# The opening of a Linformer attention and maxout FFN kernel: another form of one projection, other places for two sums, and loads cut in halves

## The chip, the cores and the metric

The kernel runs on one core of a Trainium2 chip. A core has five engines that work beside each other, each through its own instructions in order: TensorE (PE; loading its weights has a row of its own, PEld), VectorE (DVE), ScalarE (ACT), GpSimd (POOL) and SyncE (SP). The last two issue most of the DMAs here. TensorE writes into PSUM, which this kernel treats as eight banks of 128 x 512 f32. The metric is device time in microseconds, the median over runs.

## The reference, cut to what matters

```python
k_proj = np.einsum('ks,bhsd->bhkd', E, k)
v_proj = np.einsum('ks,bhsd->bhkd', F, v)
scores = scale * np.matmul(q, k_proj.transpose(0, 1, 3, 2))
attn = softmax(scores)            # over the 64 projected places
x = (attn @ v_proj)               # heads side by side: 8192 x 512
h = np.maximum(np.maximum(x @ w1, x @ w2), x @ w3)
out = h @ w_out
```

There are 8 batches, 8 heads, a sequence of 1024 and a head dimension of 64. E and F project the sequence onto 64 places. The FFN goes from 512 to 768 and back to 512. Inputs and outputs are f32.

## The kernel before, in words

**Tiling.** The sequence is split as 128 partitions by 8 places (`SI`), the heads into four pairs (`g` = 0 to 3), the 512 columns of x into the same four pieces (`ct`, one for each pair of heads), and the 768 of the FFN into six (`jt`). A batch has two chunks of 512 rows (four of the eight places each). For a chunk, x transposed (`xT`) times a weight gives a product of 128 x 512: 3 weights x 6 `jt` x 4 `ct` = 72 products (`up_mm`, L668), followed by 24 products with `w_out` (L776).

**Order.** The order on every engine is the order of the Python calls; nothing is rescheduled (`manual_schedule`, L60). A planner's clock (`clock`, `pe`, `runs`, `at`) does no more than choose PSUM banks: `bank` and `two` take those that by its count come free first. What it gets wrong turns into a wait of TensorE for the engine that still reads the bank.

**The opening, batch 0** (L631 to L661, then `up_first`, L681). The inputs come in pieces, through GpSimd's DMA queue, in the order of use: q and k by halves of the heads, v by pairs, then the weights by pieces of `ct`. Idle products (`idle`) keep TensorE busy meanwhile. `k_duo(u)` projects k for two pairs of heads: eight matmuls of 64 rows out and 256 columns (L575), copied by VectorE, and `kt_duo(u)` turns the result with two transposes (L588) and copies it into `kpT`. `v_pair(g)` projects v for one pair (L601). `exps` of `scores` (L221, L232) gives the unnormalized weights `pT`; `z(g)` adds them up (`sums`, L241) and inverts the sums on ScalarE as exp(-ln) (L301, L307); `x(g)` multiplies `pT` with v (L241 again) and scales by the inverse on VectorE into `xT` (L318). The first half of the sequence (`C0`) goes this way, pair by pair; the second half goes through `Duo` later, inside the FFN's products.

`up_first` runs the products of the first weight with `ct` outermost, so that pieces of x can be used as they come: (0, ct, jt) for ct 0 and 1 with jt 0 to 3, then both with jt 4 and 5, then ct 2 and 3. The dictionary handed to it says which attention step follows which product, for instance (before):

```python
(0, 0, 1): [lambda: x(1)],
(0, 0, 3): [lambda: z(2), lambda: z(3)],
(0, 1, 1): [lambda: v_pair(2)],
(0, 1, 3): [lambda: x(2)],
(0, 1, 5): [lambda: v_pair(3), ld(1)],
```

**Loads of the later batches.** `load(b, which)` (L198) issues one DMA for each of q, k and v of a batch, 1 MB each as landed in bf16, on GpSimd's queue. `q_t` has two buffers, `k_t` and `v_t` one, so k of batch 1 waits until batch 0's projections have read theirs. `qd(b)` packs q (copies on VectorE or ScalarE) and has SyncE issue DMAs that transpose it into `qT` (L424). For batch 1 `qd` is called twice, by two pairs each. `kproj(1)` and `vproj(1)` (through `proj`, L355, two column tiles of 64) and the scores of batch 1 stand in chunk 1 of batch 0, as `plan(0)` has them.

Of the kernel before, what the change touches and what calls it, by code (L numbers as in the profile page):

```python
# [9 lines left out]
BF16 = mybir.dt.bfloat16  # L10
# [5 lines left out]
def kernel(  # L16
# [13 lines left out]
    nc = tc.nc  # L30

    B, H, S, D = q.shape
# [5 lines left out]
    P = 128  # L38
    HALF = 64
    SI = 8  # L40
# [5 lines left out]
    SPC = SI // NCHUNK  # L46
# [5 lines left out]
    att = ctx.enter_context(tc.tile_pool(name="att", bufs=2))  # L52
# [18 lines left out]
    def deal(ns):  # L71
        clock["pe"] = max(clock["pe"], *(free[n] for n in ns))
        for n in ns:
            assert free[n] < OPEN
            free[n] = OPEN

    def two():
        n = min(range(0, 8, 2), key=lambda n: max(free[n:n + 2]))
        deal((n, n + 1))
        return psum_t[:, n:n + 2, :], (n, n + 1)  # L80

    def bank():
        n = min(range(8), key=lambda n: free[n])
        deal((n,))
        return psum_t[:, n, :], (n,)

    def pe(dt, wait=0.0):
        clock["pe"] = max(clock["pe"], wait) + dt
        return clock["pe"]

    def runs(eng, ready, dt, ns=()):
        if eng in clock:
            clock[eng] = max(clock[eng], ready + 0.06) + dt
            for n in ns:
                free[n] = clock[eng]
            return clock[eng]
        return ready + dt
# [3 lines left out]
    def copy(eng, o, i, ns=(), dt=0.65):  # L101
        done = {  # L102
            "v": nc.vector.tensor_copy, "s": nc.scalar.copy, "g": nc.gpsimd.tensor_copy
        }[eng](out=o, in_=i)
        runs(eng, clock["pe"] if ns else 0.0, dt, ns)
        return done

    def after(dma, earlier):
        tc.add_manual_dep(
            dma.ins, earlier.ins.name,  # L110
            mybir.DependencyInfo(
                mybir.DependencyClass.Sync, mybir.DependencyReason.DATA
            ),
        )


    def view(src, b):
        return src[b].rearrange("h (p si) d -> p h si d", si=SI)


    ident = const.tile([P, P], BF16, name="ident")
# [9 lines left out]
    qkv, qTs, kpTs, vps, pTs, zis, xTs = {}, {}, {}, {}, {}, {}, {}  # L131
# [5 lines left out]
    def load_tiles(b):  # L137
        qkv[b] = tuple(
            loads.tile([P, H, SI, D], BF16, name=nm, bufs=n)
            for nm, n in (("q_t", 2), ("k_t", 1), ("v_t", 1))  # L140
        )
        return qkv[b]
# [37 lines left out]
    for hp in range(2):  # L180
        for c in range(2):
            at = hp * 16 + c * 8
# [12 lines left out]
    load_w(2, slice(2, 4))  # L195
    nc.gpsimd.dma_start(out=wout_sb, in_=moe_w_out.rearrange("(jt p) m -> p jt m", p=P))

    def load(b, which):  # L198
        tiles = qkv[b] if b in qkv else load_tiles(b)
        for i in which:  # L200
            dma = nc.gpsimd.dma_start(out=tiles[i], in_=view((q, k, v)[i], b))  # L201
            if i == 0 and b - 1 in last_T:
                after(dma, last_T[b - 1])
            if i == 0 and b - 1 in turned:
                after(dma, turned[b - 1])

    def k_pair(b, g):
        if b in turned:
            return kpTs[b][:, g % 2, (g // 2) * KP:(g // 2 + 1) * KP]
        return kpTs[b][:, g, :]  # L210
# [3 lines left out]
    def scores(b, g, lo, nsi):  # L214
        t, ns = two()
        n = nsi // 2
        for c in range(2):
            for hp in range(2):
                rows = slice(hp * HALF, (hp + 1) * HALF)
                at = g * SI + lo + c * n  # L220
                nc.tensor.matmul(  # L221
                    out=t[c * HALF:(c + 1) * HALF, hp, 0:n * P],
                    lhsT=k_pair(b, g)[rows],
                    rhs=qTs[b][rows, at:at + n, :],
                    start=True, stop=True,
                )
        return t[:, :, 0:n * P], ns, pe(n * MM / 4 + 0.1)

    def exps(b, g, lo, nsi, sc):
        t, ns, ready = sc  # L230
        pTs[b, g, lo] = att.tile([P, 2, CHUNK], BF16, name="pT", bufs=6)[:, :, 0:nsi * HALF]
        nc.scalar.activation(out=pTs[b, g, lo], in_=t, func=AF.Exp, scale=scale)  # L232
        runs("s", ready, 0.17 + nsi * 0.107, ns)
# [117 lines left out]
    def proj(b, kv, t, heads, width):  # L351

        for si in range(SI):
            for hh in range(2):
                nc.tensor.matmul(  # L355
                    out=t[hh * HALF:(hh + 1) * HALF, 0:width],
                    lhsT=efT[:, si, (kv - 1) * KP:kv * KP],
                    rhs=qkv[b][kv][:, heads[hh], si, :],
                    start=(si == 0), stop=(si == SI - 1),
                )  # L360
        pe(8 * (width * 0.00042 + 0.01))
# [180 lines left out]
    def idle(n, w=warm):  # L542

        t, ns = bank()
        for _ in range(n):
            nc.tensor.matmul(out=t, lhsT=w[:, 0:P], rhs=w, start=True, stop=True)  # L546
        free[ns[0]] = pe(n * MM * (4 if w is warm_f else 1))
# [19 lines left out]
    def at(us):  # L567
        clock["pe"] = max(clock["pe"], us)

    kp0 = {}  # L570

    def k_duo(u):
        t, ns = bank()
        for si in range(SI):
            nc.tensor.matmul(  # L575
                out=t[0:KP, 0:4 * D], lhsT=efT[:, si, 0:KP],
                rhs=k_t[:, 4 * u:4 * u + 4, si, :],
                start=(si == 0), stop=(si == SI - 1),
            )
        pe(0.9)  # L580
        kp0[u] = att.tile([KP, 4 * D], BF16, name="kp0")
        copy("v", kp0[u], t[0:KP, 0:4 * D], ns, 0.45)

    def kt_duo(u):
        t, ns = bank()
        t = t.bitcast(BF16)
        for gg in range(2):
            nc.tensor.transpose(  # L588
                out=t[:, gg * KP:(gg + 1) * KP],
                in_=kp0[u][:, gg * P:(gg + 1) * P], identity=ident[0:KP, 0:KP],  # L590
            )
        pe(0.15)
        copy(
            "v", kpTs[0][:, 2 * u:2 * u + 2, :].rearrange("a g k -> a (g k)"),
            t[:, 0:2 * KP], ns, 0.25,
        )

    def v_pair(g):
        t, ns = bank()
        for si in range(SI):  # L600
            nc.tensor.matmul(  # L601
                out=t[:, 0:2 * D], lhsT=efT[:, si, KP:3 * KP],
                rhs=v_t[:, 2 * g:2 * g + 2, si, :],
                start=(si == 0), stop=(si == SI - 1),
            )
        pe(0.5)
        copy(
            "v", vps[0][:, 2 * g:2 * g + 2].rearrange("a h d -> a (h d)"),
            t[:, 0:2 * D], ns, 0.3,
        )  # L610
# [14 lines left out]
    def z(g):  # L625
        invert(0, g, *C0, sums(0, g, *C0))

    def x(g):
        scale_x(0, g, *C0, values(0, g, *C0))
# [18 lines left out]
    z(1)  # L648
    idle(1)
    at(12.8)  # L650
    k_duo(1)
    idle(1)
    at(14.8)
    v_pair(0)
    kt_duo(1)
    x(0)
    for g in (2, 3):
        exps(0, g, *C0, scores(0, g, *C0))
    at(16.1)
    v_pair(1)  # L660
    at(17.4)  # L661

    ffn_sb = ctx.enter_context(tc.tile_pool(name="ffn_sb", bufs=2))
    hTs = {}
# [138 lines left out]
    def store_now():  # L803
        stores.pop()()

    def ld(b, which=(0, 1, 2)):
        return lambda: load(b, which)

    def plan(b):
        n = b + 1  # L810
# [59 lines left out]
    for b in range(B):  # L870
        p = plan(b)

        def behind(ch, step):
            for f in p.get((ch, step), []):
                f()

        for ch in range(NCHUNK):
            if (b, ch) == (0, 0):
                c1 = (SPC, SPC)
                up_first({  # L880
                    (0, 0, 1): [lambda: x(1)],
                    (0, 0, 3): [lambda: z(2), lambda: z(3)],
                    (0, 1, 1): [lambda: v_pair(2)],
                    (0, 1, 3): [lambda: x(2)],
                    (0, 1, 5): [lambda: v_pair(3), ld(1)],
                    (0, 2, 1): [lambda: x(3)],
                    (2, "a", 0): [pack_q(0, (0, 1), *c1)],
                    (2, "a", 1): [pack_q(0, (2, 3), *c1)],
                    (2, "a", 3): [qp(0, (0, 1), *c1)],
                    (2, "a", 5): [qp(0, (2, 3), *c1)],  # L890
                    (2, 1): [duo[0].scores],
                    (2, 4): [
                        duo[0].sums, duo[0].values, duo[1].scores, duo[0].invert,
                    ],
                })
                run_later()
                behind(0, NJT - 1)
            else:
                for step in range(NJT):
                    up(b, ch, step, lambda: behind(ch, (step, "mid")))  # L900
                    behind(ch, step)
            for tt in range(SPC):
                down(b, ch, tt, "v" if b == 0 else "s")
                behind(ch, NJT + tt)
# [30 lines left out]
```

## Time and profile before

| | |
|---|---|
| median of 4 runs | 399.07 us (398.81 to 400.12) |
| the profiled execution, by the same clock | 400.12 us |
| its span in the profile | 398.3 us |
| granted TensorE clock | 1.0 |
| first projection of k (L575) | 10.47 us |
| first FFN product (L668) | 18.15 us |
| `kproj(1)`, `vproj(1)` | 50.36 and 57.30 us |
| scores of batch 1 | 56.75 us |

Issue and landing of the loads that the text uses, from the list of DMA issues by time:

| load | issued | us to landing |
|---|---|---|
| first quarter of the first weight | 6.32 | 11.7 |
| the rest of batch 0's q | 19.05 | 12.6 |
| q of batch 1 | 22.67 | 20.2 |
| k of batch 1 | 23.87 | 23.7 |
| v of batch 1 | 25.75 | 28.9 |

In the profile's rows a matmul has a start and a duration that includes the way through the array; products that follow each other start about 0.22 us apart while each is shown with 0.38. A bracket names the idle time of the engine ahead of an instruction and what ended it. "128*64" is the part of the array that an instruction uses.

### The profile page before, as it was taken

What the parts mean: (1) busy time and instruction counts of PE and PEld (TensorE: products, weight loads), DVE (VectorE), ACT (ScalarE), POOL (GpSimd) and SP (SyncE); (2) the same over time, 40 slices, a digit from 0 to 9 for tenths busy, and PEclk for the clock granted to TensorE, in tenths of its full rate; (3) what the DMA queues carried; (4) which work ended last, traced back from release to release, by engine and by line L of the source; (5) the groups of instructions that cost most, each with busy time, mean ns of one, the idle gap of its engine ahead of it and who ended that gap; (6) DMA issues with size and microseconds to landing.
All of it is one profiled execution on the core that took longest, in us unless ns stands there. A gap on an engine that the chain in (4) does not pass through costs nothing.

```text
span 398.3 us, 5745 instructions
## 1 busy us (share of the span) xinstructions
PE 390.7 (98%) x2286; PEld 176.3 (44%) x2286; DVE 202.0 (51%) x312; ACT 152.3 (38%) x239; POOL 34.2 (9%) x49
## 2 busy tenths in 40 slices
PE   7899999999999999999999999999999999999996
PEld 3444443453445445344454445444454444444443
DVE  2348756751864535645273544745266442745251
ACT  2434638527222552253323532245323533132322
POOL 7440011000400200200002000200000000000000
PEclk9999999999999999999999999999999999999999
DMA  8999999977999999999979979696980129020203
GB/s 140 205 206 207 205 253 149 249 139 168 224 181 265 153 221 203 223 179 196 221 207 144 253 166 274 93 229 125 214 215 30 77 76 246 0 105 2 105 0 107
DMA packets 67339, 66.31 MB, mean 166 GB/s; under 512 B 31504, under 2 KB 59792, under 8 KB 67312
## 3 DMA queue, kind: packets, MB, share of 16 engines
q0 software_dynamic: 29104, 30.41, 47.7%
q1 hardware_dynamic: 38064, 35.46, 34.8%
q8 instruction: 18, 0.29, 0.3%
q10 hardware_dynamic: 144, 0.07, 0.1%
q14 instruction: 9, 0.07, 0.0%
HBM read 69.73 MB, written 16.97 MB: 218 GB/s over the span
## 4 chain that ended last, share of the span: by engine, by line
PE 90%; DMA 6%; DVE 1%; ACT 1%; issue 0%; POOL 0%; DVEq 0%; ACTq 0%; POOLq 0%
PE banks L668 60%; PE banks L776 19%; DMA qT<-q_p 4%; PE banks L355 3%; PE banks L241 2%; DMA k_t<-in_k_dram 2%; PE banks L221 2%; PE banks L266 1%; DVE xT L318 1%; ACT zi_all L307 1%; ACT zl L301 1%; PE banks L575 1%; PE banks L546 0%; PE banks L601 0%; PE banks L756 0%
## 5 line engine op out<-in xcount | busy, mean ns | idle before, releaser
L668 PE MATMUL banks<-xT,w_sb 128*128 128x512 bf16 x1152 | 257.1, 379 | 0.3 <-DVE xT L318 0.3
L668 PEld LDWEIGHTS <-w_sb 128*128 128x128 bf16 x1152 | 110.2, 98 | 136.6 <-issue 8.5
L737 DVE TENSOR_TENSOR m<-banks,h1s 128x512 f32<-128x512 f32 x90 | 62.1, 690 | 134.5 <-ACT h1s L733 90.7
L733 ACT COPY h1s<-banks 128x512 f32<-128x512 f32 x90 | 52.6, 585 | 122.2 <-PE banks L668 120.7
L776 PE MATMUL banks<-wout_sb,hT 128*128 128x512 bf16 x378 | 86.9, 380 | 0.1
L678 DVE TENSOR_TENSOR hT<-banks,m 128x512 bf16<-128x512 f32 x90 | 62.3, 692 | 9.4
L776 PEld LDWEIGHTS <-hT 128*128 128x128 bf16 x378 | 35.3, 98 | 48.2 <-issue 5.9
L102 ACT COPY o_sb<-banks 128x512 f32<-128x512 f32 (+2 forms) x57 | 32.9, 577 | 58.6 <-PE banks L776 58.1
L318 DVE TENSOR_TENSOR xT<-banks,zi_all 128x1024 bf16<-128x1024 f32 x28 | 33.2, 1220 | 11.5 <-PE banks L241 6.9
L232 ACT ACTIVATE pT<-banks 128x1024 bf16<-128x1024 f32 (+1 forms) x32 | 30.2, 975 | 15.5 <-PE banks L221 15.5
L201 POOL DMA_DIRECT2D q_t<-in_q_dram x7 | 6.1, 878 | 197.8 <-DVE xT L318 76.7
L355 PEld LDWEIGHTS <-efT 128*64 128x64 bf16 x224 | 11.6, 110 | 3.4 <-issue 3.4
L102 DVE CAST vp<-banks 64x256 bf16<-64x256 f32 (+1 forms) x18 | 7.1, 397 | 11.5 <-ACT vp L102 9.0
L102 ACT CAST vp<-banks 64x256 bf16<-64x256 f32 x14 | 5.1, 364 | 18.4 <-PE banks L355 18.3
L241 PE MATMUL banks<-pT,vp 64*64 64x512 bf16 (+1 forms) x128 | 10.3, 375 | 0.2 <-DVE vp L102 0.2
L221 PE MATMUL banks<-qT,kpT 64*64 64x512 bf16 (+1 forms) x128 | 9.7, 372 | 0.7 <-DMA qT<-q_p 0.7
L102 DVE COPY q_p<-q_t 128x1024 bf16<-128x1024 bf16 x26 | 9.8, 438 | 0.6 <-DMA q_t<-in_q_dram 0.6
L102 DVE COPY o_sb<-banks 128x512 f32<-128x512 f32 (+1 forms) x9 | 5.6, 640 | 5.4 <-PE banks L756 4.5
L546 PE MATMUL banks<-warm_f 128*128 128x512 f32 x8 | 6.6, 977 | 1.5 <-DVE warm_f L175 1.5
L301 ACT ACTIVATE zl<-banks 128x512 f32<-128x512 f32 (+1 forms) x8 | 6.5, 810 | 2.9 <-PE banks L241 2.7
L355 PE MATMUL banks<-k_t,efT 128*64 128x256 bf16 x112 | 7.5, 276 | 0.0
L355 PE MATMUL banks<-v_t,efT 128*64 128x256 bf16 x112 | 7.3, 273 | 0.0
(73 smaller groups left out, 124.3 us busy)
## 6 DMA issues: line engine op xcount, KB each, us to landing
out_dram<-o_sb SPq DMA_DIRECT2D x30, 512.0 KB, 4.5
zi_all<-zd SPq DMA_DIRECT2D x20, 512.0 KB, 7.8
q_t<-in_q_dram POOLq DMA_DIRECT2D x7, 1024.0 KB, 10.2
k_t<-in_k_dram POOLq DMA_DIRECT2D x7, 1024.0 KB, 16.6
v_t<-in_v_dram POOLq DMA_DIRECT2D x7, 1024.0 KB, 21.8
zi_all<-zd POOLq DMA_DIRECT2D x4, 512.0 KB, 7.9
w_sb<-in_moe_w_dram POOLq DMA_DIRECT2D x4, 384.0 KB, 10.4
k_t<-in_k_dram POOLq DMA_DIRECT2D x2, 512.0 KB, 9.5
```

What stands on the lines that cost most here:

```text
L102: done = {"v": nc.vector.tensor_copy, "s": nc.scalar.copy, "g": nc.gpsimd.tensor_copy}[eng](out=o, in_=i)
L221: nc.tensor.matmul(out=t[c * HALF:(c + 1) * HALF, hp, 0:n * P], lhsT=k_pair(b, g)[rows], rhs=qTs[b][rows, at:at + n, :], start=True, stop= ...
L232: nc.scalar.activation(out=pTs[b, g, lo], in_=t, func=AF.Exp, scale=scale)
L241: nc.tensor.matmul(out=t[hp * HALF:(hp + 1) * HALF, c, 0:nsi * HALF], lhsT=w(rows, hp), rhs=p[rows, hp, :], start=True, stop=True,)
L301: nc.scalar.activation(out=zl, in_=t, func=AF.Ln)
L318: nc.vector.tensor_tensor(out=xTs[b][:, g, lo:lo + nsi, :].rearrange("a (c s) p -> a c (s p)", c=2), in0=t, in1=zi, op=ALU.mult,)
L355: nc.tensor.matmul(out=t[hh * HALF:(hh + 1) * HALF, 0:width], lhsT=efT[:, si, (kv - 1) * KP:kv * KP], rhs=qkv[b][kv][:, heads[hh], si, :], ...
L668: nc.tensor.matmul(out=h, lhsT=w_sb[i][:, ct, jt * P:(jt + 1) * P], rhs=xTs[b][:, ct, ch * SPC:(ch + 1) * SPC, :], start=(ct == first), st ...
L678: nc.vector.tensor_tensor(out=o, in0=h, in1=other, op=ALU.max)
L733: nc.scalar.copy(out=h1s, in_=h[0][0])
L737: nc.vector.tensor_tensor(out=m12, in0=h[1][0], in1=h1s, op=ALU.max)
L776: nc.tensor.matmul(out=o_ps, lhsT=hTs[b, ch][:, jt, tt * P:(tt + 1) * P], rhs=wout_sb[:, jt, :], start=(jt == 0), stop=(jt == NJT - 1),)
```

## The change

Three edits. First, `k_quad` and `kt_quad` take the place of `k_duo(1)` and `kt_duo(1)` for pairs 2 and 3 of batch 0. The projection writes two pairs of heads as two column tiles of 64, the lower pair onto partitions 0 to 63, the upper onto 64 to 127, through the helper `proj`; one 128 x 128 transpose turns both. `kt_quad(1)` now stands ahead of `v_pair(0)`, and the scores of pairs 2 and 3 ahead of `x(0)`. Second, the sums `z(2)` and `z(3)` stand ahead of the first FFN product instead of behind the fourth, and `v_pair(2)`, `x(2)` follow other products: behind (0, 1, 3) and (0, 0, 5). Third, k and v of batch 1 are loaded by halves of the eight places, one DMA each; q as before. The planner's clock is set to 17.0 instead of 17.4 behind the opening.

```diff
-    def load(b, which):
+    def load(b, which, halves=False):
         tiles = qkv[b] if b in qkv else load_tiles(b)
-        for i in which:
-            dma = nc.gpsimd.dma_start(out=tiles[i], in_=view((q, k, v)[i], b))
+        for i, sis in [
+            (i, sis) for i in which
+            for sis in ((slice(0, SPC), slice(SPC, SI)) if halves else (slice(0, SI),))
+        ]:
+            dma = nc.gpsimd.dma_start(
+                out=tiles[i][:, :, sis], in_=view((q, k, v)[i], b)[:, :, sis]
+            )
...
+    def k_quad(u):
+
+        t, ns = bank()
+        proj(0, 1, t, (slice(4 * u, 4 * u + 2), slice(4 * u + 2, 4 * u + 4)), 2 * D)
+        kp0[u] = att.tile([P, 2 * D], BF16, name="kp0q", bufs=1)
+        copy("v", kp0[u], t[:, 0:2 * D], ns, 0.27)
+
+    def kt_quad(u):
+        t, ns = bank()
+        t = t.bitcast(BF16)
+        nc.tensor.transpose(out=t[:, 0:P], in_=kp0[u], identity=ident)
+        pe(0.1)
+        copy(
+            "v", kpTs[0][:, 2 * u:2 * u + 2, :].rearrange("a g k -> a (g k)"),
+            t[:, 0:P], ns, 0.25,
+        )
...
     at(12.8)
-    k_duo(1)
+    k_quad(1)
     idle(1)
+    kt_quad(1)
     at(14.8)
     v_pair(0)
-    kt_duo(1)
-    x(0)
     for g in (2, 3):
         exps(0, g, *C0, scores(0, g, *C0))
+    x(0)
     at(16.1)
     v_pair(1)
-    at(17.4)
+    z(2)
+    z(3)
+    at(17.0)
...
                     (0, 0, 1): [lambda: x(1)],
-                    (0, 0, 3): [lambda: z(2), lambda: z(3)],
-                    (0, 1, 1): [lambda: v_pair(2)],
-                    (0, 1, 3): [lambda: x(2)],
-                    (0, 1, 5): [lambda: v_pair(3), ld(1)],
+                    (0, 1, 3): [lambda: v_pair(2)],
+                    (0, 0, 5): [lambda: x(2)],
+                    (0, 1, 5): [lambda: v_pair(3), ld(1, (0,)), ld(1, (1, 2), True)],
                     (0, 2, 1): [lambda: x(3)],
```

More of the change, by code (lines that the diff above doesn't have):

```diff
@@ L804, in store_now, with ld @@
         stores.pop()()
-    def ld(b, which=(0, 1, 2)):
-        return lambda: load(b, which)
+    def ld(b, which=(0, 1, 2), halves=False):
+        return lambda: load(b, which, halves)
     def plan(b):
```

## The prediction

> **What bounds the kernel now.** I read the page first: which engine fills the span, and whether its clock is whole.
>
> ```profile
> PE 390.7 (98%) x2286; PEld 176.3 (44%) x2286; DVE 202.0 (51%) x312; ACT 152.3 (38%) x239; POOL 34.2 (9%) x49
> ...
> PEclk9999999999999999999999999999999999999999
> DMA  8999999977999999999979979696980129020203
> ```
>
> TensorE is the bound at full clock, so a change can only gain where TensorE starts late or stands still. Going through the starts of its matmuls, I find all standing still longer than 0.15 us past about 24 us to be 2 us in sum; the largest piece, 0.86 us at 166, is a wait for a transposing DMA. The rest of the edit's ground is the opening. The chain of waits says where it turns solid:
>
> ```profile
> 17.31 0.70 DVE xT L318
> ...
> 19.10 0.70 DVE xT L318
> ...
> 24.05 9.23 PE banks L668 x42
> ```
>
> Before 24 us the chain alternates between engines; from 24.05 on 42 FFN products stand back to back. So the edits of the opening are worth what they do to the start of that block. Its timeline, TensorE alone and then VectorE alone (start, us busy, engine, line, tiles):
>
> ```profile
> 18.15 0.59 PE L668 MATMUL banks<-xT,w_sb 128*128 128x512 bf16 x2 [0.17 <-DVE xT L318]
> 18.68 0.30 PE L241 MATMUL banks<-pT,vp 64*64 64x256 bf16 x4
> 18.91 0.60 PE L668 MATMUL banks<-xT,w_sb 128*128 128x512 bf16 x2
> 19.45 0.70 PE L241 MATMUL banks<-pT,ones 64*64 64x256 bf16 x8
> 20.08 0.60 PE L668 MATMUL banks<-xT,w_sb 128*128 128x512 bf16 x2
> 20.52 0.61 PE L601 MATMUL banks<-v_t,efT 128*128 128x128 bf16 x8
> ...
> 21.59 0.30 PE L241 MATMUL banks<-pT,vp 64*64 64x256 bf16 x4
> ...
> 22.76 0.61 PE L601 MATMUL banks<-v_t,efT 128*128 128x128 bf16 x8
> ```
> ```profile
> 17.31 0.69 DVE L318 TENSOR_TENSOR xT<-banks,zi 128x512 bf16<-128x512 f32 x1 [0.35 <-PE banks L241]
> ...
> 19.10 0.69 DVE L318 TENSOR_TENSOR xT<-banks,zi 128x512 bf16<-128x512 f32 x1 [0.79 <-PE banks L241]
> ...
> 22.01 0.69 DVE L318 TENSOR_TENSOR xT<-banks,zi 128x512 bf16<-128x512 f32 x1 [0.48 <-PE banks L241]
> ```
>
> The reader is to see a hidden cover: pair 1's x is ready at 19.10 + 0.69 = 19.79, and the FFN products that need it start at 20.08. TensorE fills that gap with the sums of pairs 2 and 3 (19.45).
>
> **The second k half.** Removed: 8 matmuls of 256 columns (start 14.67, 1.06 us), a 64x256 copy (0.42) and two turns. Added: 16 matmuls of 128 columns in two column tiles, a 128x128 copy (0.29, the row of vp) and one 128x128 turn. No row has these 16. Nearest are the transposes of q_t (L366): also 128 rows by 64 columns, 128 columns moving, 16 in 0.64 us. The other end is L355's 16 of 256 columns, 1.06 us. I take 0.64: the copy starts about 0.1 us behind, 15.42, ends 15.71, the turn runs at 15.76, its kpT copy ends 16.25 instead of 16.96. v_pair(0) now stands behind the turn: it moves from 15.89 to about 15.83, so vp, x(0) and pair 0's xT move by only 0.06 us, to 17.25–17.94. The exps of pairs 2 and 3 start at 16.70 instead of 17.37. By the other end v_pair(0), and all behind it, is 0.36 us later. That is the hitch: the half is quicker, but v's projection waited for none of it and now waits for its copy and turn.
>
> **Sums moved ahead.** The eight sums leave 19.45 and stand ahead of the first FFN product. Those of pair 2 run in the wait for xT. Those of pair 3 take the two banks that x(0) held, so they wait until pair 0's xT is read (17.94): they start at 18.0 and the products 0.22 us behind their last start (as 19.86 to 20.08 in the old order), at 18.25 instead of 18.15. Sooner than 18.15 is not to be had: w0's first quarter lands at 6.32 + 11.7 = 18.02. Ln and exp of the sums run earlier on ScalarE; x(2) and x(3), which want them, come at 21.6 and later, so that is worth nothing.
>
> Then the cover is gone. x(1) goes out 0.53 us behind the first product (as 18.15 to 18.68), its xT is done 1.11 us later (18.68 to 19.79), and the next FFN products, (1,0) to (1,3), stand directly there with nothing between, and TensorE works in order, so all its products wait behind: 18.25 + 0.53 + 1.11 + 0.06 = 19.95, after about 0.5 us of standing still. Four of them at 0.216 us come before v_pair(2), which the diff moves behind (0,1,3): 20.82 against 20.52. From v_pair(2) to the block of 42 the chain is the old one: vp's copy, x(2), xT, v_pair(3) (it takes the banks that xT reads, in both orders), vp, x(3). In the old order 20.52 to 23.98; the products laid between its links (two fewer now, 14 ahead of the block in both orders) run beside VectorE's work and don't lengthen it. So the block starts 0.30 us **later**. With 18.15 in place of 18.25 it is 0.20, with L355's price for k about 0.7. Below zero: only if x(2) didn't wait for v_pair(2), which both orders exclude. I take **+0.30**.
>
> Behind 24 us nothing gives it back: the block is solid, and the q_p copies that feed the turns at 33.12 were ready by 32.8 (landing 19.05 + 12.6 = 31.65, then two copies), about 0.5 us of slack that a later TensorE doesn't need. A gain, had there been one, would have ended there.
>
> **k and v of batch 1 in halves.** SP sees nothing new; POOL issues four instead of two DMAs, at 0.88 us each. The lanes shift by two: v's second half waits for w2's first landing, 18.14 + 10.9 = 29.0, instead of issuing at 25.75. Ahead of it in the queue stands work until 47 us, so the later issue costs nothing. k's projection takes the halves one behind the other, and so does v's. Cost of the smaller packets (512 B landed instead of 1024 B), from the windows (busy columns of each engine, clock, DMA share, GB/s):
>
> ```profile
> 28.40:30.40 2.00, 2.00 (x11) 0.94 (x10) 0.90 (x2) 0.00 (x0) 0.00 (x0) 1.00 1.45 198
> ...
> 40.00:42.00 2.00, 2.00 (x24) 0.86 (x22) 1.20 (x2) 1.90 (x3) 0.00 (x0) 1.00 1.23 207
> 48.00:51.00 3.00, 3.00 (x24) 1.53 (x23) 2.61 (x4) 0.61 (x2) 0.00 (x0) 1.00 1.21 195
> 51.00:54.00 3.00, 3.00 (x21) 1.38 (x18) 1.22 (x3) 0.58 (x1) 0.00 (x0) 1.00 1.30 155
> ```
>
> 28.4–30.4 is the rest of batch 0's q, in just such half rows: 198 GB/s. 40–42 is full rows: 207. For 2.1 MB that is 10.6 us against 10.1, **+0.5 us**. Here the Trainium skill speaks against the change (DMA: Bandwidth & Descriptors, Rules for kernel authors and Anatomy of one DMA): at least 1 MiB per DMA for full bandwidth, with some 2.0 us fixed for each. By that rule two more DMAs cost up to 4 us, v would land at 54.65 + 4 = 58.7, and its second half is wanted at 57.30 + 0.3 + 0.5 = 58.1: +0.6 us on the path. By the row it lands near 55.2 and costs nothing. I take the row, since in a queue with 20 us of backlog the fixed parts overlap.
>
> k lands at 23.87 + 23.7 = 47.6 and is wanted at 50.36; v at 54.65 and wanted at 57.30. Nothing waits for either now, so the halves can gain nothing.
>
> What they can disturb is the turned q of batch 1: two transposing DMAs issued from 44.08, moving packets from 48 us beside v's load. In 50 to 51 us the two queues moved 153 and 150 packets: one for one. v's 1024 packets become 2048, so the transposes share with it longer. Their first half landed at 44.08 + 11.9 = 55.98; the scores of batch 1 want it at 56.75, slack 0.77. With everything 0.3 us later and the packets one for one at 42 ns (512 B at 198 GB/s over 16 engines) + 25 ns, v and the first half both move until about 56.4, landing near 57.1 against a want of 57.05. If the engines are only shared by bytes, it lands at 56.3 and no one waits. Ends 0 and 0.4; I take **+0.12**, nearer the one-for-one row than its extreme.
>
> **Sum.** 0.30 + 0.12 = +0.42 us. The span goes from 398.3 to 398.7, that profiled execution's 400.12 (1.8 us outside its span) to 400.5, and the median from 399.07 to **399.5 us**. About 0.3%, 1.2 us, is what a measurement here can tell from no change; the forecast is inside it.
>
> **Rivals.**
> - *The transposes come late (slower).* In 51–54 us, where v's end and the second transpose meet, only 155 GB/s were moved against 195: 0.6 us of work lost. With twice the packets for v that stretch could last 6 us instead of 3, and the first half would land at 57.7 to 58.5 rather than 57.1. The price is what lies past 57.05, 0.7 to 1.5 us on top of +0.30: 400.1 to 400.9, say 400.5. It decides from a landing past 58.0. For it: batch 4's scores already stood 0.86 us for such a transpose. Against: the byte rates fall little with small packets.
> - *The sums' slot is a true gain (faster, a little).* If (1,0) need not wait and the sums' 0.72 us (19.14 to 20.08 less a product) drop out, the stage gains 0.6, cut to 0.5 by the q_p copies: 398.6. Against: xT's 0.69 us row, and w0's landing at 18.02.
> - *That gain, and the 0.86 us wait at 166 goes too* because loads and transposes meet in another phase: 399.07 - 0.5 - 0.86 = 397.7. Little speaks for it: those loads are issued relative to TensorE's own steps.
> - *The halves do nothing, as nothing waited:* then +0.30 alone, 399.4, inside the forecast's own range.
>
> **Numbers.** Forecast with its own range 398.9 to 400.1: 0.48. Late transposes: 0.30. Small gain: 0.12. Gain and wait gone: 0.10. Slower by over 0.3% takes most of the second case and a little of the first, 0.33; faster the fourth and the scatter of the third, 0.13; the rest 0.54. Range 398.3 to 401.0: it leaves out the fourth case and the ends of the second.
>
> **What would show it.** Right: first FFN product at 18.2 to 18.3; a wait of some 0.5 us for xT ahead of the fifth product; v_pair(2) near 20.8; the solid block from about 24.3; v's second half landing near 55–57; the scores of batch 1 near 57.1. Wrong: the block starting before 24.0; the projection of k or v waiting for a DMA; the scores past 57.8, which is the first rival; or a TensorE clock below 1.0 after 15 us.

## The result, and the profile after

| | before | after |
|---|---|---|
| median | 399.24 us (398.58 to 400.52, 64 runs) | 400.22 us (399.40 to 401.18, 43 runs) |
| the profiled execution | 400.12 us | 399.71 us |
| its span | 398.3 us | 397.9 us |

The ratio is 1.0024, with an interval of 1.0019 to 1.0028: 0.98 us slower, where the forecast was 0.42 us. That is inside the 0.3% taken as no change, and in the direction forecast. The two profiled executions stand the other way round, 0.41 us in favour of the changed kernel. So the first thing to settle is which steps of a single trace stand for all executions.

The page of the changed kernel, engines and DMA by slices:

```profile
PE 390.0 (98%) x2293; PEld 175.9 (44%) x2293; DVE 201.7 (51%) x312; ACT 152.3 (38%) x239; POOL 36.1 (9%) x51
...
PEclk9999999999999999999999999999999999999999
DMA  9999999987999999999979979696990139020203
```

Nothing here tells of a loss: the clock is whole and TensorE as full as before. The opening, TensorE alone (start, us busy, engine, line, tiles; the lines of the FFN products moved from L668 to L692, those of v's projection from L601 to L623):

```profile
13.94 0.64 PE L360 MATMUL banks<-k_t,efT 128*64 128x128 bf16 x16
...
15.03 0.23 PE L599 MATMUL banks<-ident,kp0q 128*128 128x128 bf16 x1
15.10 0.61 PE L623 MATMUL banks<-v_t,efT 128*128 128x128 bf16 x8
...
17.50 0.60 PE L692 MATMUL banks<-xT,w_sb 128*128 128x512 bf16 x2
...
19.27 1.04 PE L692 MATMUL banks<-xT,w_sb 128*128 128x512 bf16 x4 [0.39 <-DMA w_sb<-in_moe_w_dram]
20.14 0.61 PE L623 MATMUL banks<-v_t,efT 128*128 128x128 bf16 x8
...
22.30 0.61 PE L623 MATMUL banks<-v_t,efT 128*128 128x128 bf16 x8 [0.33 <-DVE xT L323]
...
23.53 9.30 PE L692 MATMUL banks<-xT,w_sb 128*128 128x512 bf16 x42
```

The reader is to see a wait of the forecast size ahead of the fifth product (19.27), and that the solid block nevertheless starts at 23.53, 0.45 us earlier than in the profile of before. Everything in this execution, from the k half on (13.94 against 14.67), stands earlier.

The loss lies later. These are the projection of k, the scores and the projection of v of batch 1, TensorE's timeline of before and then of after:

```profile
50.36 1.06 PE L355 MATMUL banks<-k_t,efT 128*64 128x256 bf16 x16
56.75 0.63 PE L221 MATMUL banks<-qT,kpT 64*64 64x512 bf16 x8
57.30 1.06 PE L355 MATMUL banks<-v_t,efT 128*64 128x256 bf16 x16
```
```profile
49.91 1.06 PE L360 MATMUL banks<-k_t,efT 128*64 128x256 bf16 x16
57.10 0.63 PE L226 MATMUL banks<-qT,kpT 64*64 64x512 bf16 x8 [0.73 <-DVE hT L702]
57.65 1.06 PE L360 MATMUL banks<-v_t,efT 128*64 128x256 bf16 x16
```

From k's projection to the scores TensorE has fixed work: 6.39 us before, and 7.19 us after, 0.80 us of standing still. The bracket names VectorE's hT, since that ends as the scores start:

```profile
56.41 0.69 DVE L702 TENSOR_TENSOR hT<-banks,m 128x512 bf16<-128x512 f32 x1
```

But the scores don't need it. In the changed kernel with whole loads (the first experiment) they start at 57.12, ahead of the same step of VectorE (TensorE's row, then VectorE's):

```profile
57.12 0.63 PE L226 MATMUL banks<-qT,kpT 64*64 64x512 bf16 x8
57.23 0.69 DVE L702 TENSOR_TENSOR hT<-banks,m 128x512 bf16<-128x512 f32 x1
```

What they do need, and what came last of that, is a transposing DMA: the first half of batch 1's turned q was issued at 43.86 and took 13.1 us, so it landed at 56.96; before it was issued at 44.08 and took 11.9, landing at 55.98. In all four later profiles in which TensorE stands still at this place the bracket names this DMA itself. v's own projection waits for nothing, and follows the scores in 0.55 us in both.

One more difference explains the profiled spans: the wait of 0.86 us for a transposing DMA at 166 us, which the prediction counted as the largest piece, stands in the profile of before. Of the eleven others one has a wait there at all (the change again, 0.26 us in its bracket, where before's bracket has 0.70). Its size belonged to that execution. Without it, and with an earlier opening, the profiled execution of after is shorter although its median is longer.

### The profile page after: what moved, and what is told of

Read it like the earlier page. It is cut to its first block, busy times and chain, and to the rows that moved or that the text cites. A ratio compares the mean times of both kernels' runs of the same rounds, so it can differ in the third digit from the quotient of the medians.

```text
span 397.9 us, 5761 instructions
## 1 busy us (share of the span) xinstructions
PE 390.0 (98%) x2293; PEld 175.9 (44%) x2293; DVE 201.7 (51%) x312; ACT 152.3 (38%) x239; POOL 36.1 (9%) x51
## 4 chain that ended last, share of the span: by engine, by line
PE 90%; DMA 3%; DVE 2%; POOL 1%; ACT 1%; issue 1%; DVEq 0%; ACTq 0%; POOLq 0%
PE banks L692 61%; PE banks L800 20%; PE banks L360 3%; DMA w_sb<-in_moe_w_dram 3%; PE banks L246 2%; PE banks L226 2%; DVE xT L323 1%; PE banks L271 1%; DVE hT L702 1%; ACT zi_all L312 1%; ACT zl L306 1%; DVE m L761 0%; POOL k_t L152 0%; POOL q_t L157 0%; POOL v_t L152 0%
## 5 line engine op out<-in xcount | busy, mean ns | idle before, releaser
L692 PE MATMUL banks<-xT,w_sb 128*128 128x512 bf16 x1152 | 257.1, 379 | 0.5 <-DMA w_sb<-in_moe_w_dram 0.4
L692 PEld LDWEIGHTS <-w_sb 128*128 128x128 bf16 x1152 | 110.2, 98 | 137.2 <-issue 8.5
L102 ACT COPY o_sb<-banks 128x512 f32<-128x512 f32 (+2 forms) x57 | 32.9, 577 | 57.7 <-PE banks L800 57.2
L323 DVE TENSOR_TENSOR xT<-banks,zi_all 128x1024 bf16<-128x1024 f32 x28 | 33.1, 1220 | 11.5 <-PE banks L246 6.9
L102 DVE CAST vp<-banks 64x256 bf16<-64x256 f32 (+1 forms) x18 | 7.1, 396 | 12.4 <-ACT vp L102 9.8
L360 PE MATMUL banks<-k_t,efT 128*64 128x256 bf16 (+1 forms) x128 | 8.1, 269 | 0.0
L204 POOL DMA_DIRECT2D v_t<-in_v_dram x8 | 7.1, 892 | 2.0 <-DMA w_sb<-in_moe_w_dram 2.0
```

The lines of the kernel that those rows point to most:

```text
L102: done = {"v": nc.vector.tensor_copy, "s": nc.scalar.copy, "g": nc.gpsimd.tensor_copy}[eng](out=o, in_=i)
L204: dma = nc.gpsimd.dma_start(out=tiles[i][:, :, sis], in_=view((q, k, v)[i], b)[:, :, sis])
L323: nc.vector.tensor_tensor(out=xTs[b][:, g, lo:lo + nsi, :].rearrange("a (c s) p -> a c (s p)", c=2), in0=t, in1=zi, op=ALU.mult,)
L360: nc.tensor.matmul(out=t[hh * HALF:(hh + 1) * HALF, 0:width], lhsT=efT[:, si, (kv - 1) * KP:kv * KP], rhs=qkv[b][kv][:, heads[hh], si, :], ...
L692: nc.tensor.matmul(out=h, lhsT=w_sb[i][:, ct, jt * P:(jt + 1) * P], rhs=xTs[b][:, ct, ch * SPC:(ch + 1) * SPC, :], start=(ct == first), st ...
```

## The experiments

Open after the first reading were three things: whether the loss comes from the opening or from the halves; if from the halves, whether the size of the packets, the number of DMAs or a lower byte rate makes it; and why the forecast's +0.30 us of the opening doesn't show. Each run was timed against before on the same chip.

**The edits of the opening alone.** The changed kernel, with k and v of batch 1 loaded whole:

```diff
-(0, 1, 5): [lambda: v_pair(3), ld(1, (0,)), ld(1, (1, 2), True)],
+(0, 1, 5): [lambda: v_pair(3), ld(1)],
```

> The changed kernel with k and v of batch 1 loaded whole, as before: the edits of the opening alone. Theory 1 (two costs: the opening's chain, and the transposes of batch 1's q, which share the DMA engines packet for packet with v's load): from the first matmul of the second k half to the block of 42 products 9.6 us, as in the changed kernel (before 9.3); the first matmul of batch 1's scores stands at most 0.2 us longer than a plain switch; time over before by 0.3 us. Theory 2 (the opening makes all of the loss, the scores' wait was the chance of one execution): over before by 1.0 us.

Measured: 399.06 us against 398.99, ratio 0.9997 (0.9989 to 1.0005). The forecast's +0.30 us, which was also expected here, would be 1.0008, and lies outside. From k's projection to the scores it is 6.39 us again, with the transpose back at 11.9 us.

**The halves alone.** Before, with k and v of batch 1 each in two DMAs by sequence halves. `load` was given a list of pieces for batch 1; the other batches are as before (`cut` names the pieces by 0 for q, 1 for k, 2 for v; the edit is written shorter here than in the kernel, and so are the ones that build on it):

```diff
-        for i in which:
-            dma = nc.gpsimd.dma_start(out=tiles[i], in_=view((q, k, v)[i], b))
+        whole = [(ALL, slice(0, SI))]
+        S2 = [(ALL, slice(0, SPC)), (ALL, slice(SPC, SI))]
+        cut = {1: S2, 2: S2} if b == 1 else {}
+        for i, hs, sis in [(i, hs, sis) for i in which for hs, sis in cut.get(i, whole)]:
+            dma = nc.gpsimd.dma_start(
+                out=tiles[i][:, hs, sis], in_=view((q, k, v)[i], b)[:, hs, sis]
+            )
```

> The kernel before with nothing changed but k and v of batch 1 in sequence halves. Theory 1: the opening takes 9.3 us as before; in 48 to 55 us the two queues move about 240 packets each per us; the first transpose lands near 57 us and the scores wait 0.3 to 0.9 us; time over before by 0.5 to 0.8 us. Theory 2: no difference from before.

Measured: 400.37 us against 398.99, ratio 1.0031 (1.0020 to 1.0041). The whole loss is here, and more than the 0.5 to 0.8 us expected. The transpose takes 13.5 us and the scores stand 7.36 us behind k's projection instead of 6.39.

**v in quarters.** The same, with v in four pieces of two places (256 B packets), and k whole:

```diff
-cut = {1: S2, 2: S2} if b == 1 else {}
+cut = {2: [(ALL, slice(n, n + 2)) for n in range(0, SI, 2)]} if b == 1 else {}
```

> The kernel before with v of batch 1 in four sequence quarters (256 B packets as landed, 4096 of them), k whole: the suspected packet count doubled once more. Theory 1 (one packet for one): a round is now 25 + 25 ns, so the transposes get more of the engines than with halves: their first half lands by about 55.5, the scores do not wait, and instead v's last quarter lands past 60 us and v's projection waits 2 to 3 us; time over before by 2 to 3 us. Rival (small packets slow both alike): the first transpose lands later than with halves, past 58 us, and the scores wait 1.5 us or more.

Measured: 403.52 us against 398.99, ratio 1.0112 (1.0089 to 1.0136), more than the 2 to 3 us expected, and by another wait than in the halves. The queues between 49 and 50 us show why (queue, packets, MB, share of the 16 engines): first after, then this kernel. q0 is GpSimd's queue, here v's load; q1 is SyncE's, here the transposes.

```profile
q0 software_dynamic: 237, 0.12, 84.6%
q1 hardware_dynamic: 240, 0.06, 45.8%
```
```profile
q0 software_dynamic: 335, 0.08, 82.6%
q1 hardware_dynamic: 335, 0.09, 64.4%
```

Before has 154 and 154 in the same microsecond. In all three the two queues move the same **number** of packets, whatever the packets' sizes. So a quicker round (both packets 256 B) lets the transposes go faster, 335 packets instead of 154, while v gets fewer bytes: 0.08 MB instead of 0.16. The first half of the turned q landed at 55.93 and the scores wait for nothing (6.39 us again), and v is the one that is late, its last quarter at 31.80 + 28.3 = 60.10. TensorE's timeline:

```profile
56.30 0.63 PE L226 MATMUL banks<-qT,kpT 64*64 64x512 bf16 x8
56.86 0.85 PE L360 MATMUL banks<-v_t,efT 128*64 128x256 bf16 x12
60.16 0.41 PE L360 MATMUL banks<-v_t,efT 128*64 128x256 bf16 x4 [2.45 <-DMA v_t<-in_v_dram]
60.50 3.80 PE L673 MATMUL banks<-xT,w_sb 128*128 128x512 bf16 x9
```

The reader is to see 2.45 us of waiting for v's last quarter, and then nine products in 3.80 us: starts 0.43 apart instead of 0.22. The windows show the cause (us, busy of PE, PEld, DVE, ACT, POOL, granted clock, DMA share, GB/s):

```profile
58.00:60.00 2.00, 0.00 (x0) 0.00 (x0) 0.00 (x0) 0.00 (x0) 0.00 (x0) 1.00 1.37 119
...
61.20:62.20 1.00, 1.00 (x4) 0.35 (x3) 0.79 (x2) 0.16 (x1) 0.86 (x1) 0.50 1.00 410
...
64.20:65.20 1.00, 1.00 (x12) 0.36 (x14) 0.88 (x2) 0.00 (x0) 0.00 (x0) 1.00 0.98 77
```

The granted clock is 0.50 for some 3.5 us behind the wait. That is 8 products at 0.21 us more, 1.7 us; with the wait some 4.1 of the 4.5 us measured (an estimate from this one profile). The timed runs go with it: five of the six have a mean clock of 0.992 to 0.996, and the sixth, at 1.000, is the quickest with 402.13 us.

**As many DMAs, with full packets.** Before, with k and v of batch 1 each in two DMAs by halves of the heads, so that rows stay 1024 B:

```diff
-cut = {1: S2, 2: S2} if b == 1 else {}
+HD = [(LO, slice(0, SI)), (HI, slice(0, SI))]
+cut = {1: HD, 2: HD} if b == 1 else {}
```

> The kernel before with k and v of batch 1 in two DMAs each by halves of the heads: as many DMAs as the change, but packets of 1024 B as before. Theory 1 (packets count, not DMAs): first transpose lands near 56 us, no wait at the scores, no difference from before within 0.15 us. Rival (each further DMA costs some 2 us of its own, as the Trainium skill has it under DMA: Bandwidth & Descriptors, Anatomy of one DMA): v lands 2 to 4 us later, past 57.3, and the time is over before by 0.5 us or more.

Measured: 399.33 us against 398.99, ratio 1.0002 (0.9993 to 1.0011). Its one trace has the transpose at 12.9 us and 0.34 us of waiting, where none was expected, but over 14 runs the time is that of before (the interval reaches from 0.3 us less to 0.4 us more). The two DMAs more cost nothing that can be measured; the smaller packets, in the runs that follow, do.

**v alone and k alone in sequence halves,** on before:

```diff
-cut = {1: S2, 2: S2} if b == 1 else {}
+cut = {2: S2} if b == 1 else {}
```

> The kernel before with v of batch 1 alone in sequence halves, k whole. Theory (only the load that moves beside the transposes matters, and that is v): all of the loss of both halved, over before by 0.9 to 1.4 us; the scores of batch 1 wait 0.6 to 1.2 us. Rival (both loads' lower rate adds up): half of it, 0.6 us.

```diff
-cut = {1: S2, 2: S2} if b == 1 else {}
+cut = {1: S2} if b == 1 else {}
```

> The kernel before with k of batch 1 alone in sequence halves, v whole. Theory: k is through before the transposes move packets at 48 us, so it costs no more than its later end of some 0.25 us: over before by 0 to 0.3 us. Rival (both loads' lower rate adds up): 0.6 us.

Measured: v alone 400.22 us against 399.20, ratio 1.0021 (1.0012 to 1.0029); k alone 399.19, ratio 1.0003 (0.9992 to 1.0014). v alone gives the loss of the change. Its trace is the cleanest of all, since it happens to run as the profile of before does up to this point (k's projection at 50.36 in both, the transposes issued at 44.08 in both):

```profile
50.36 1.06 PE L360 MATMUL banks<-k_t,efT 128*64 128x256 bf16 x16
58.13 0.63 PE L226 MATMUL banks<-qT,kpT 64*64 64x512 bf16 x8 [1.31 <-DMA qT<-q_p]
```

Here the bracket names the transposing DMA. It took 13.9 us instead of 11.9, landed at 57.98, and the scores start 1.38 us later than in before. That fits k's halves, which do nothing: k has landed (25.70 + 22.2 = 47.90) before the transposes move more than single packets, at 48.

**The parts of the opening.** First the new k half alone: the changed kernel with whole loads and the sums, `v_pair(2)` and `x(2)` in their old places (the lines on the loads are left out here).

```diff
-    z(2)
-    z(3)
-    at(17.0)
+    at(17.4)
...
-(0, 1, 3): [lambda: v_pair(2)],
-(0, 0, 5): [lambda: x(2)],
+(0, 0, 3): [lambda: z(2), lambda: z(3)],
+(0, 1, 1): [lambda: v_pair(2)],
+(0, 1, 3): [lambda: x(2)],
```

> The changed kernel with whole loads and the sums of pairs 2 and 3, v_pair(2) and x(2) at their old places: the new k half alone. Theory (the opening runs at the pace of the landings of v and of the first weight, so its order is worth little): within 0.3 us of before. The prediction's rival reading (v's projection, now behind the turn, delays the chain): over before by 0.2 us or more, and from the second k half to the block of 42 products longer than before's 9.3 us although nothing waits for a DMA.

And the reverse, the sums, `v_pair(2)` and `x(2)` in the new places in before, with the old k half and whole loads (the diff above, turned round):

> The kernel before (old k half, whole loads) with the sums of pairs 2 and 3 ahead of the first products and v_pair(2), x(2) at their new places. The prediction's step: the cover of xT's 0.69 us is gone, so a wait of about 0.5 us stands ahead of the fifth product and the time is over before by 0.2 to 0.4 us. Theory after the first runs: the wait is there, but in the old order v_pair(2) waits for its load at the same place, so the time is within 0.3 us of before.

Measured: 399.43 us for the k half, ratio 1.0002 (0.9992 to 1.0013), and 399.28 us for the sums, ratio 0.9999 (0.9989 to 1.0010). Neither alone does anything that can be measured, and together they don't either. Why shows in the start of `v_pair(2)`. With the old order of the sums, the halves alone (TensorE) and the new k half alone (loading of weights):

```profile
20.37 0.62 PE L606 MATMUL banks<-v_t,efT 128*128 128x128 bf16 x8 [0.42 <-DMA v_t<-in_v_dram]
```
```profile
20.16 0.45 PEld L623 LDWEIGHTS <-efT 128*128 128x128 bf16 x8 [0.88 <-DMA v_t<-in_v_dram]
```

There `v_pair(2)` waits for the load of v's third pair itself. With the new order the edits of the opening alone show the same: the load landed at 7.46 + 13.5 = 20.96, and

```profile
20.97 0.61 PE L623 MATMUL banks<-v_t,efT 128*128 128x128 bf16 x8
...
24.36 0.82 PE L692 MATMUL banks<-xT,w_sb 128*128 128x512 bf16 x3
```

Over all twelve profiles (landing from the list of DMA issues, starts from the timeline):

| order of the sums | third pair of v lands | `v_pair(2)` behind it | the solid block behind it |
|---|---|---|---|
| old: before | 20.26 | 0.26 | 3.72 |
| old: six other kernels | 20.02 to 20.51 | 0.01 to 0.06 | 3.47 to 3.53 |
| new: after | 19.85 | 0.29 | 3.68 |
| new: sums alone | 19.66 | 0.28 | 3.67 |
| new: three others | 19.69 to 20.96 | 0.01 to 0.07 | 3.40 to 3.45 |

In nine of twelve the load decides, in both orders. There the new order is not slower but a little quicker: from the start of `v_pair(2)` to the block it is 3.38 to 3.39 us in all five profiles of the new order and 3.46 to 3.47 in the seven of the old one. Between the profiles the landing moves by 1.3 us, and between the two of the changed kernel itself by 1.1 (19.85 and 20.96), more than either edit was priced at; what makes it early or late was not found.

**The change mended, and the change again.** If v's packets are the cause, then v whole should take the loss away with all else of the change kept:

```diff
-(0, 1, 5): [lambda: v_pair(3), ld(1, (0,)), ld(1, (1, 2), True)],
+(0, 1, 5): [lambda: v_pair(3), ld(1, (0,)), ld(1, (1,), True), ld(1, (2,))],
```

> The changed kernel with one part undone: v of batch 1 loaded whole, everything else as changed (k in halves, the new opening). Theory after the first eight runs (v's packets beside the transposes are the whole loss): no difference from before within 0.3 us, no wait ahead of batch 1's scores beyond a plain switch. Rival (the new opening and the halves cost only together, since the opening moves TensorE against the loads): over before by 0.5 us or more.

> The changed kernel once more, on the same chip as the run with v whole: over before by 0.8 to 1.2 us; the first transpose of batch 1's q takes 13 us or more from issue to landing and the scores wait 0.6 to 1.5 us. If the scores do not wait in this second execution, the wait in the first was chance and the loss lies elsewhere.

Measured on one chip: 398.80 us with v whole, and 399.86 for the change as it was, against 399.04 for before. The ratios are 0.9994 (0.9984 to 1.0004) and 1.0023 (1.0015 to 1.0031). The mended kernel has the scores 6.39 us behind k's projection, and the change 7.44. One load left whole is worth 1.06 us, which is the whole loss. The mended kernel is not shown to be faster than before: its interval holds 1.

## Why the prediction was right, and which term was off

The forecast of no change that can be told, with a small loss, came out. Its sum did so in part by luck: 0.30 of the 0.42 us stood on the opening, which costs nothing that can be measured, and the 0.12 us of the transposes is the term that makes the whole loss of about 1 us.

**The new k half: right.** It took the 0.64 us of the row chosen. From its start to the turn is 13.94 to 15.03, 1.09 us, and to `v_pair(0)` 1.16: both as worked out.

**The chain of the opening: right within one execution, wrong as a cost.** From the k half to the first FFN product was to be 3.58 us and is 3.56; from there to `v_pair(2)` 2.57 and is 2.64; from `v_pair(2)` to the block 3.46 and is 3.39. From the k half to the block that makes 9.59, against 9.31 in before and the 9.61 of the forecast. Yet the opening alone costs nothing that can be measured (its interval reaches from 0.4 us less to 0.2 us more). The step that failed here is "From `v_pair(2)` to the block of 42 the chain is the old one" as the link that carries +0.30 into the time: it took `v_pair(2)` to be held by TensorE's order, at 20.52. The load it needs had landed at 20.26, 0.26 us earlier, and the prediction has no landing for it. In the other six profiles of the old order `v_pair(2)` starts within 0.06 us of that landing. Before's is the one of the seven in which the order held `v_pair(2)`, and not the load.

By the prediction's own test, a block that starts before 24.0, the profile of after (23.53) refutes the +0.30. The test itself was poor: with the same opening the block starts at 24.36 and 24.41 in two other profiles (whole loads; the change again) and at 23.10 in a third (v whole). An absolute time within the opening can't judge steps of 0.3 us where the loads move by 1.3.

The wait ahead of the fifth product came out at the forecast size (0.39 us in the bracket, 0.55 from start to start), though the profile puts it down to the second quarter of the first weight. That was issued at about 7.0 and took 12.2 us, landing at about 19.2, and xT was ready at 18.46 + 0.69 = 19.15: here the two can't be told apart, so the size is no proof of the cause that was forecast. The landing of the first quarter, 18.02, was misread: 11.7 us is the median of the two quarters, and the first took 11.5 and landed at 17.82. Nothing in the sum hangs on it, since the first product of before waits for pair 0's xT until 17.31 + 0.69 = 18.00.

The scores at 57.10, where "near 57.1" was the forecast's sign of being right, met that number by luck: the opening stood 0.45 us earlier than in before, and the wait is 0.80 us.

**The transposes: the place and the sharing right, the size off.** The row of packets one for one was the right one to read: 237 and 240 packets in a microsecond, where 42 ns + 25 ns make 239. And the transposes do share with v's load longer. By 53 us they had even moved more packets than in before (975 against 857, counted from 48 us). They fall behind from 53 to 56 us, with 1179 packets against 2032, where v's load still has 382 of its own to move, against 42 in before. v's second half landed at 28.99 + 27.4 = 56.39 against "until about 56.4", and the first half of the turned q at 56.96 against 57.1. The term that was mis-sized is "+0.12", of which 0.05 was the bare landing behind the want and the rest a margin. Measured in the profile of after: 0.80. Three pieces account for the difference:

- The transpose took 13.1 us from its issue, where the forecast had 57.1 - 44.38 = 12.7: 0.4 us.
- The scores start 0.14 us behind the landing (56.96 to 57.10; 57.98 to 58.13 with v alone). The forecast had no such step.
- The scores were due 49.91 + 6.39 = 56.30, 12.44 us behind the issue of the transposes, where the forecast had 12.67: 0.23 us. This piece comes with the new order of the sums. From the issue of the transposes to k's projection it is 6.02 to 6.05 us in its five profiles, and 6.27 to 6.28 in the seven of the old order. The transposes are issued behind VectorE's copies of q (43.30 + 0.75 = 44.05 and 44.08 in before), and beside TensorE these come 0.23 us later in the changed kernel. So the edit of the opening took 0.23 of the slack of 0.77 us. In the mended kernel the first half landed at 43.43 + 12.3 = 55.73, only 0.14 us ahead of the scores at 55.87.

0.05 + 0.4 + 0.14 + 0.23 = 0.82. In the four profiles with v in sequence halves the transposes take 13.1, 13.3, 13.5 and 13.9 us; in the five with v whole and the loads not cut by heads, apart from before, 11.8 to 12.4. The slack of 0.77 us was read from one execution, and a spread of 0.8 us in the transposes is as large as that slack. The waits of these four (0.80, 0.97, 1.05, 1.38 us, mean 1.05) lie in the same range as their medians, 0.82 to 1.38 us above before.

**Rule and row.** By the rule that the prediction set aside (the Trainium skill, DMA: Bandwidth & Descriptors, Rules for kernel authors and Anatomy of one DMA), two more DMAs were to make v land at 58.7 by its estimate, and its projection wait. v landed at 56.39, and its projection waited for nothing; two more DMAs with full packets give 1.0002. So in this backlogged queue no fixed cost for each DMA shows in the time. The halves do cost time, but to another queue than the one that carries them.

**The rivals.** "The transposes come late" comes close to what happened. Its wait of 0.7 to 1.5 us is the size measured, and its stretch of low rate did go on: the windows from 54 to 56 us of before and then of after (the last column is GB/s)

```profile
54.00:56.00 2.00, 2.00 (x12) 0.95 (x11) 0.94 (x3) 0.58 (x1) 0.00 (x0) 1.00 1.27 227
```
```profile
54.00:56.00 2.00, 2.00 (x11) 0.88 (x9) 0.98 (x3) 0.58 (x1) 0.00 (x0) 1.00 1.43 146
```

go with the packets of v's load in these two microseconds: 10 in before and 158 in after. What it had wrong is the +0.30 of the opening beneath it, and its landings of 57.7 to 58.5: two of four lie there (57.98 with v alone, 58.06 in the change again), 56.96 and 57.44 don't. The forecast took the smaller of two sizes of one mechanism; how the 0.4 us of longer transposes divide between the packets' count and the slow stretch was not separated. Sharing one for one is not all of it: from 55 to 56 us in after the transposes moved 388 packets beside only 33 of v's, where before moved 742 beside 10 from 54 to 55. "The halves do nothing, as nothing waited" is refuted by the halves alone, 1.0031. A gain in the opening is not shown, and the 0.86 us at 166 us was no property of the kernel, so the last rival had nothing to win.

## What to carry to other kernels

A load that nobody waits for is not free to be cut into smaller packets: look up which other queue moves packets in the same stretch, count packets and not only bytes, and compare with the slack of whoever waits for that queue. An edit elsewhere can have taken part of that slack. Before an edit of the order is priced from one profile, check for every instruction of the chain when its load landed. Where that is within a few tenths of its start, the order is worth little, and a second profile of the same kernel tells more than a second reading of the first.

## What the hardware showed unexpectedly

- Between 49 and 50 us two backlogged queues were served packet for packet: 154 to 154 with 1024 B beside 256 B, 237 to 240 with 512 B beside 256 B, 335 to 335 with 256 B beside 256 B. Smaller packets in one made that queue slower (0.16, 0.12 and 0.08 MB in that microsecond), but its neighbour didn't follow in one direction: with quarters the transposes landed as early as in before (55.93 and 55.98), with halves 1 to 2 us later (56.96 to 58.06).
- Behind a wait of 2.45 us the granted clock fell to 0.50 for some 3.5 us, while behind waits of up to 1.31 us it stayed at 1.00. The Trainium skill (TensorE: Matmul & The Clock Gate, Part 1: The HAM clock gate) has the drop to half behind an idle window of about 3.4 us; here a shorter wait was enough.
- In the stretch of the transposes, from 48 to 57 us, each of the twelve profiles has at least one microsecond in which all queues together move only 14 to 100 GB/s, where the microseconds in which both queues share at full pace have 170 to 210. In after it lies between 50 and 51 us, with 100 and 107 packets instead of 237 and 240:

```profile
DMA packets 207, 0.08 MB, mean 79 GB/s; under 512 B 107, under 2 KB 207, under 8 KB 207
...
q1 hardware_dynamic: 107, 0.03, 109.1%
q0 software_dynamic: 100, 0.05, 103.5%
```

No run was made to tell what it is, and it stays open, as do its second spell in several profiles (in after the 421 packets from 55 to 56 us) and what moves the landings of the opening's loads by over a microsecond from one execution to the next.
